# Loading wq with one transfer of 32 KB rows in place of two of 16 KB rows, and issuing the output store from ScalarE

## The chip, the cores and the metric

The kernel runs on one core of a Trainium2 chip. The metric is device time in microseconds (us), the median of several executions; lower is better. "Span" is the profiled part of one execution, about 1.9 us shorter than the device time.

In the profiles PE is the matmul unit of TensorE, DVE is VectorE, ACT ScalarE and SP SyncE; q1, q8 and q10 are the DMA queues of SyncE, of the instructions and of ScalarE. A wait marked "issue" is one for nothing that the profile shows. A stretch is called warm where TensorE's granted clock is full, and cold where it is half.

## The reference, cut to what matters

One decode step of a conditioned transformer block for 4 sequences: six modulation vectors from `c` and `w_mod`, layer norm, a q projection, attention of 32 query heads over the last 1024 positions of 8 key/value heads, an output projection, then a feed-forward block.

```python
mod = (silu(c) @ w_mod).reshape(4, 6, 1, 512)         # w_mod 512 x 3072, 3 MB
h = layernorm(x) * (1 + ca) + sa
q = h @ wq                                            # wq 512 x 4096, 4 MB
p = softmax(q @ k.T * 128 ** -0.5)                    # k, v: 8 MB each
x = x + ga * ((p @ v) @ wo)                           # wo 4096 x 512, 4 MB
h = layernorm(x) * (1 + cb) + sb
x = x + gb * (relu(h @ w1) @ w2)                      # w1, w2: 1.8 MB each
```

Nearly all of it is 32 MB of bfloat16 that is read once.

## The kernel before

All large loads go out from SP (SyncE) in the order in which they are needed. The parts that matter here, with cuts:

```python
for gi in range(KAHEAD):                  # KAHEAD = 2: k0, k1
    load_k(gi)
wmod_sb = wts.tile([P, DT, 6 * D], bf16, tag="med", name="wmod_sb")
nc.sync.dma_start(out=wmod_sb[:], in_=w_mod.rearrange("(p t) n -> p t n", t=DT))
wq_sb = wts.tile([P, DT, Hq * Dh], bf16, tag="big", name="wq_sb")
wq_src = A_wq.rearrange("(p t) n -> p t n", t=DT)
for t in range(0, DT, 2):
    nc.sync.dma_start(out=wq_sb[:, t:t + 2, :], in_=wq_src[:, t:t + 2, :])
for gi in range(KAHEAD, NG):              # k2 .. k7
    load_k(gi)
# ... v0 .. v7, wo in four, w1, w2 in five transfers

for t in range(DT):                       # q projection, 128 matmuls; t = 0, 1 read the first half
    for hq in range(Hq):
        nc.tensor.matmul(out=qT_v[:, hq, :], lhsT=wq_sb[:, t, hq * Dh:(hq + 1) * Dh], rhs=hT[:, t, :],
                         start=(t == 0 and hq == 0), stop=(t == DT - 1 and hq == Hq - 1))
# ... scores of k0, k1; transposes and scores of k2 .. k7; softmax; p @ v; wo; feed-forward
nc.vector.tensor_tensor(out=res[:], in0=zg[:], in1=x12_ps[:], op=ALU.add)
nc.sync.dma_start(out=out.rearrange("b o (g n) -> (o g) b n", g=NH), in_=res[::BS, :])
```

The transfers take their completion semaphores from a ring of eight. So each transfer from the ninth on waits until the one eight places before it has landed, and the issue times on SP show landings.

## Time and profile before

| | before |
|---|---|
| device time, median (lowest to highest) | 85.89 us (85.84 to 86.03, 3 runs) |
| span | 84.0 us |
| DMA queue of SP: bytes, share of 16 engines | 31.99 MB, 91.9% |
| PE, VectorE, ScalarE busy | 68%, 31%, 28% |
| last landing, as the start of the last matmuls of z | 80.16 us |
| res ready to the end of the span | 2.60 us |

The lines for the load stream, the chain and q are in the prediction below. The first is the page's row of TensorE's granted clock (one digit for each of 40 slices of 2.1 us, in tenths of full speed):

```profile
PEclk9999999858955555999999995795555555555555
```

The clock falls to half (5) near 18 us. The store in the timeline of SP (start, duration):

```profile
81.47 0.69 SPq L483 DMA_DIRECT2D out_dram<-res  x1
```

### The profile page before, as it was taken

Reading aid. Unit: us, or ns where it says so; the run is one execution under the profiler, and the core shown is the slowest. Engines: PE = TensorE matmul, PEld = TensorE weight load, DVE = VectorE, ACT = ScalarE, POOL = GpSimd, SP = SyncE. Lnnn points to the kernel's source line nnn. Section 1 sums busy time; section 2 is a strip of 40 time slices with the busy share of each in tenths; the row PEclk is TensorE's granted clock in tenths of the full one; section 3 lists DMA queues with packets and bytes.
Section 4 is the critical chain, followed back from the end, with each engine's and each line's share of the span. In section 5 each row is a group of like instructions: output and inputs, shape, how many; then the busy total and the mean of one; then the engine's idle time right before and its main releaser. Section 6 shows DMA issues by size and latency. Waiting matters only on the chain.

```text
span 84.0 us, 2368 instructions
## 1 busy us (share of the span) xinstructions
PE 57.2 (68%) x1064; PEld 46.8 (56%) x1064; DVE 26.3 (31%) x73; ACT 23.5 (28%) x37; POOL 5.2 (6%) x20
## 2 busy tenths in 40 slices
PE   0039930599629899999999239996455478598730
PEld 0039920238529749977777039996452058588510
DVE  0145470030430103654666677500003020241320
ACT  2314760003020004977789096300000010011000
POOL 6980000000000000000000000000000000000000
PEclk9999999858955555999999995795555555555555
DMA  0999998999989999999999999999999999999600
GB/s 2 329 406 452 456 480 374 429 444 429 437 374 417 417 441 409 409 413 433 425 406 413 425 429 417 409 425 429 413 409 413 429 419 443 417 376 401 236 4 2
DMA packets 4221, 32.14 MB, mean 382 GB/s; under 512 B 492, under 2 KB 628, under 8 KB 1140
## 3 DMA queue, kind: packets, MB, share of 16 engines
q1 hardware_dynamic: 4196, 31.99, 91.9%
q8 instruction: 8, 0.13, 0.6%
q10 hardware_dynamic: 16, 0.01, 0.0%
q14 instruction: 1, 0.01, 0.0%
HBM read 31.99 MB, written 0.00 MB: 381 GB/s over the span
## 4 chain that ended last, share of the span: by engine, by line
DMA 92%; SPq 2%; PE 1%; DVE 1%; issue 0%
DMA v<-in_A_v_cache_dram 28%; DMA wo_sb<-in_A_wo_dram 24%; DMA wq_sb<-in_A_wq_dram 21%; DMA w<-in_B_w_dram 19%; SPq L81 1%; PE z_ps L470 1%; SPq L90 1%; DVE zg L480 0%; DVE res L482 0%
## 5 line engine op out<-in xcount | busy, mean ns | idle before, releaser
L207 ACT COPY kT<-ktp 128x1024 bf16<-128x1024 bf16 x16 | 15.5, 1016 | 12.7 <-PE ktp L202 11.7
L202 PEld LDWEIGHTS <-k 128*128 128x128 bf16 x256 | 17.0, 108 | 3.7 <-issue 2.5
L202 PE MATMUL ktp<-ident_k,k 128*128 128x128 bf16 x256 | 18.0, 238 | 1.1 <-DMA k<-in_A_k_cache_dram 1.1
L205 DVE COPY kT<-ktp 128x1024 bf16<-128x1024 bf16 x16 | 11.1, 691 | 11.1 <-PE ktp L202 10.8
L340 PE MATMUL oT_ps<-pT,v 128*128 128x16 bf16 x256 | 7.3, 172 | 2.5 <-issue 1.9
L340 PEld LDWEIGHTS <-v 128*128 128x128 bf16 x256 | 7.1, 100 | 2.7 <-issue 2.0
L214 PE MATMUL sc_ps<-kT,qpad 128*32 128x512 bf16 x64 | 5.6, 445 | 0.4 <-DVE qpad L306 0.4
L357 PE MATMUL pT_ps<-ident_bf,p_rep 128*128 128x128 bf16 x32 | 3.3, 289 | 2.9 <-DVE p_rep L351 2.9
L357 PEld LDWEIGHTS <-p_rep 128*128 128x128 bf16 x32 | 2.9, 135 | 3.4 <-DVE p_rep L351 3.2
L236 PE MATMUL m_ps<-wmod_sb,siluT 128*32 128x512 bf16 x16 | 1.5, 516 | 4.5 <-DMA wmod_sb<-in_w_mod_dram 4.5
L302 PE MATMUL qT_ps<-hT,wq_sb 128*128 128x4 bf16 x128 | 3.6, 166 | 1.4 <-DVE ab L295 1.4
L302 PEld LDWEIGHTS <-wq_sb 128*128 128x128 bf16 x128 | 3.5, 104 | 1.5 <-issue 1.5
L409 ACT COPY y<-y_ps 128x256 f32<-128x256 f32 x1 | 0.4, 372 | 11.4 <-DVE y L408 11.4
L404 PE MATMUL y_ps<-wo_sb,o 128*32 128x512 bf16 x16 | 2.1, 620 | 2.0 <-DMA wo_sb<-in_A_wo_dram 1.1
L177 PE MATMUL tp<-ident_bf,cx_sb 8*128 8x8 bf16 x4 | 0.3, 167 | 4.5 <-DMA cx_sb<-in_A_x_dram 4.5
L236 PEld LDWEIGHTS <-siluT 128*32 128x32 bf16 x16 | 0.4, 107 | 4.8 <-issue 4.6
L382 DVE TENSOR_TENSOR oT_sb<-oT_ps,rb 128x128 bf16<-128x128 f32 x1 | 0.3, 292 | 8.6 <-PE oT_ps L340 8.6
L416 PEld LDWEIGHTS <-wo_sb 128*128 128x128 bf16 x64 | 2.5, 120 | 0.6 <-DMA wo_sb<-in_A_wo_dram 0.6
L416 PE MATMUL y_ps<-o,wo_sb 128*128 128x4 bf16 x64 | 2.4, 173 | 0.5 <-DMA wo_sb<-in_A_wo_dram 0.5
L351 DVE TENSOR_TENSOR p_rep<-e_sb,mi 128x512 int32<-128x512 int32 x4 | 2.5, 686 | 0.7 <-ACT e_sb L346 0.7
L470 PE MATMUL z_ps<-w,uT 128*32 128x128 bf16 x56 | 2.2, 302 | 0.7 <-DMA w<-in_B_w_dram 0.5
L177 PEld LDWEIGHTS <-cx_sb 8*128 8x128 bf16 x4 | 0.2, 108 | 4.5 <-issue 4.5
(107 smaller groups left out, 56.1 us busy)
## 6 DMA issues: line engine op xcount, KB each, us to landing
k<-in_A_k_cache_dram SPq DMA_DIRECT2D x8, 1024.0 KB, 26.2
v<-in_A_v_cache_dram SPq DMA_DIRECT2D x8, 1024.0 KB, 19.9
wq_sb<-in_A_wq_dram SPq DMA_DIRECT2D x2, 2048.0 KB, 20.7
wo_sb<-in_A_wo_dram SPq DMA_DIRECT2D x4, 1024.0 KB, 19.9
wmod_sb<-in_w_mod_dram SPq DMA_DIRECT2D x1, 3072.0 KB, 13.5
w<-in_B_w_dram SPq DMA_DIRECT2D x1, 1792.0 KB, 21.7
w<-in_B_w_dram SPq DMA_DIRECT2D x2, 512.0 KB, 19.2
w<-in_B_w_dram SPq DMA_DIRECT2D x1, 384.0 KB, 17.8
```

The lines of the kernel that those rows point to most:

```text
L202: nc.tensor.transpose(out=tp[:, ii, :], in_=k_tiles[gi][:, iq * IQ + ii, :], identity=ident_k)
L205: nc.vector.tensor_copy(out=dst, in_=tp[:])
L207: nc.scalar.copy(out=dst, in_=tp[:])
L214: nc.tensor.matmul(out=sc_ps[hw * CG:(hw + 1) * CG, half * HALF:(half + 1) * HALF], lhsT=qpad[:, b, par, hw, :], rhs=kT[:, half * (NI // 2 ...
L236: nc.tensor.matmul(out=m4_ps[k * CG:(k + 1) * CG, :], lhsT=siluT32[:, t, :], rhs=wmod_sb[:, t, k * D:(k + 1) * D], start=(t == 0), stop=(t ...
L302: nc.tensor.matmul(out=qT_v[:, hq, :], lhsT=wq_sb[:, t, hq * Dh:(hq + 1) * Dh], rhs=hT[:, t, :], start=(t == 0 and hq == 0), stop=(t == DT ...
L340: nc.tensor.matmul(out=oT_ps[:, hw, par].rearrange("p b r -> p (b r)"), lhsT=v_tiles[h][:, i, :], rhs=pT[:, i, c0:c0 + B * rep], start=(fi ...
L351: nc.vector.tensor_tensor(out=p_w[:, ws, :], in0=e_w[:, ws].unsqueeze(2).to_broadcast([P, WQ // 2, B]), in1=mi4[:].unsqueeze(1).to_broadca ...
L357: nc.tensor.transpose(out=tp[:, ii, :], in_=p_rep[:, i // 2, :, i % 2], identity=ident_bf[:])
L404: nc.tensor.matmul(out=y4_ps[q0:q0 + CG, :], lhsT=o4[:, l, g % 2, g // 2, :], rhs=wo_sb[:, g, l, :], start=(g == 0 and l < 4), stop=(g == ...
L416: nc.tensor.matmul(out=y_ps[:, m, :], lhsT=wo_sb[:, g, l, m::DT], rhs=o4[:, l, g % 2, g // 2, 0:B], start=False, stop=(g == NP - 1 and l = ...
L470: nc.tensor.matmul(out=z_ps[nh * CG:(nh + 1) * CG, :], lhsT=uT32[:, m, :], rhs=w2_sb[:, m, nh * DH2:(nh + 1) * DH2], start=(m == 0), stop= ...
```

## The change

The intent: larger rows mean fewer pieces for the DMA engines and one issue less on SP; and ScalarE, idle at the end, issues the store.

```diff
-    for t in range(0, DT, 2):
-        nc.sync.dma_start(out=wq_sb[:, t:t + 2, :], in_=wq_src[:, t:t + 2, :])
+    nc.sync.dma_start(out=wq_sb[:], in_=wq_src)
...
-    nc.sync.dma_start(out=out.rearrange("b o (g n) -> (o g) b n", g=NH), in_=res[::BS, :])
+    nc.scalar.dma_start(out=out.rearrange("b o (g n) -> (o g) b n", g=NH), in_=res[::BS, :])
```

Lines after the edit move up by one: L302 of the kernel before is L301 of the changed one.

## The prediction

> **What bounds the kernel now.** I read the row of 40 slices and the queue totals first, then the chain of waits in order of time, then the waits of the DMA queue, then the timelines around wq and at the end.
>
> ```profile
> DMA  0999998999989999999999999999999999999600
> ...
> q1 hardware_dynamic: 4196, 31.99, 91.9%
> q8 instruction: 8, 0.13, 0.6%
> ```
>
> The 16 DMA engines are busy in every slice from the second to the 37th. 91.9% of 84.0 us is 77.2 us of packet time, and it lies between 2.0 us (first k tile) and 80.0 us (last piece of w2), so there is hardly any hole in the stream. PE, at 68%, is not the bound.
>
> ```profile
> 2.71 17.78 DMA wq_sb<-in_A_wq_dram
> ...
> 20.50 23.76 DMA v<-in_A_v_cache_dram
> ...
> 44.28 19.86 DMA wo_sb<-in_A_wo_dram
> ...
> 64.16 15.96 DMA w<-in_B_w_dram
> ...
> 80.16 0.64 PE z_ps L470 x10
> ...
> 80.83 0.30 DVE zg L480
> ...
> 81.15 0.29 DVE res L482
> ```
>
> This is the chain that ended last: four stretches of the load stream, 77.4 us, then the last ten matmuls, two VectorE operations and the store. So only two things can move the end: how long the load queue takes for its 32 MB, and what happens after the last load has landed (80.12 us) until 84.0 us. Both parts of the change touch one of these, each by little.
>
> The size of a row's own cost comes from the issue times on SP. A load waits for the one eight places before it in the order of issue, so a start shows a landing:
>
> ```profile
> 8.30 0.54 SPq L81 DMA_DIRECT2D k<-in_A_k_cache_dram  x1
> 15.60 0.54 SPq L81 DMA_DIRECT2D k<-in_A_k_cache_dram  x1
> 20.50 0.54 SPq L101 DMA_DIRECT2D v<-in_A_v_cache_dram  x1
> 26.89 0.54 SPq L101 DMA_DIRECT2D v<-in_A_v_cache_dram  x1
> 54.22 0.33 SPq L119 DMA_DIRECT2D w<-in_B_w_dram  x1
> 56.70 0.33 SPq L125 DMA_DIRECT2D w<-in_B_w_dram  x1
> ```
>
> These are six answers of the timeline of SP (start, duration). The first four are released by k1, wmod, the first wq half and the second wq half; the last two by v4 and v5.
>
> **What the Trainium skill says.** (1) "DMA: Bandwidth & Descriptors", section "Issuing engines are not separate DMA queues": transfers from ScalarE and SyncE run on the same 16 engines, and another issuer only saves the sequencer's issue time. The trace agrees as far as it goes: the two small loads of ScalarE are its own queue (q10, 16 packets), and the engines are one pool. At the end SP's sequencer is idle, waiting 12.3 us for res, so there is no issue time to save. (2) The same page, "Latency and other measured facts", gives about 600 ns for the first byte of such a transfer. In the trace the store's issue ends at 82.16 us and its first packets begin in 82.70 to 82.80 us: about 0.6 us, agreed. (3) "Perfetto Trace Analysis", "DMA Instruction — HWDGE (DVE, Sync)": the profiled span of an issue is the wait for the descriptor generator's lock, its use, and the push of semaphores, and data movement is not in it. The store's 0.69 us is such a span. (4) "TensorE: Matmul & The Clock Gate", Part 1: the clock is at half until about 3.4 us of steady work. The trace shows a clock of 0.50 from 23 to 33.8 us and 1.00 after. This bears on a delay of PE below.
>
> **Part 1, wq in one transfer.** Removed: one issue on SP (two issues took 1.07 us together, one should take about 0.55), 128 of 256 row packets, one semaphore write per engine. The bytes stay.
>
> An engine carries 128/16 = 8 rows of each transfer. From the starts: v4 to v5 is 56.70 - 54.22 = 2.48 us for 8 rows of 8 KB, 310 ns a row. The first wq half is 20.50 - 15.60 = 4.90 us for 8 rows of 16 KB, 612 ns a row. wmod is 15.60 - 8.30 = 7.30 us for 8 rows of 24 KB, 912 ns. So 8 KB more costs some 301 ns, and about 10 ns is the row's own. One row of 32 KB is then 310 + 3 x 301 = 1213 ns against 2 x 612 = 1224 ns. Saved per engine: 8 x 11 = 0.09 us, and with one semaphore write less some 0.1 us. As the stream has no holes this comes off every later landing, down to the last of w2: -0.1 us on the path.
>
> The 0.5 us of SP issue is not on the path: the third, fourth and later loads are issued while k0 is still moving (k0 and k1 land at about 5.5 and 8 us; wq is issued at 2.7 us and starts to move only when wmod is through, after 15 us).
>
> The order of issue is otherwise the same. v0 now waits for wmod and not for the first wq half, so it goes out some 5 us earlier, and everything from v1 on waits for the same load as before. The queue holds seven or eight loads, some 18 us of work, so neither matters.
>
> **What part 1 costs PE.** Before, the 64 q matmuls of t=0,1 read the first half and run while the second half arrives:
>
> ```profile
> 25.20:26.90 1.70, 1.70 (x64) 1.70 (x64) 0.50 0.99 414
> 26.90:28.80 1.90, 1.88 (x70) 1.80 (x67) 0.50 0.99 414
> ```
>
> These two stretches are of line 302 only. The second half is seen landed at 26.89 us, exactly when the 65th matmul begins. With one semaphore for 4 MB none may start before about 26.8 us. So the q projection runs 26.8 to 30.4 us in place of 25.2 to 28.8: PE's whole chain is 1.6 us later. If the warm clock comes a window later too, up to 3.4 us more run at half clock, 1.7 us lost, 3.3 us in all. I looked for where this is given back:
>
> ```profile
> PE oT_ps L340 <- issue: 1.9, 1, 1.9
> PE y_ps L404 <- DMA wo_sb<-in_A_wo_dram: 1.1, 1, 1.1
> ...
> PE oT_ps L340 <- DMA v<-in_A_v_cache_dram: 0.6, 1, 0.6
> ```
>
> Between 58 and 67 us PE is idle 1.9 us before v6's work, 0.6 us for v7 and 1.1 us for the second piece of wo, 3.6 us together. After it wo, w1 and w2 pace PE anew (0.5, 0.4 and 0.3 us of waits), so the end does not see the delay. The k tiles' buffers come free later too, but v5 (issued at about 36.9 us) needs k2's transposes, done by about 33.5 us; and a late issue would eat from a queue of 18 us.
>
> **Part 2, the store from ScalarE.** Before: res is done at 81.44 us, the issue begins at 81.47 and takes 0.69 us, packets begin 0.6 us later, and the program ends at 84.0. The issue, the flight and the closing barrier (2.5 us) are all on the path. ScalarE's last operation starts at 75.73 us, so it is idle and waits there. Its own issues in this trace are these:
>
> ```profile
> 0.73 0.55 ACTq L71 DMA_DIRECT2D cx_sb<-in_c_dram  x1
> 1.31 0.26 ACTq L72 DMA_DIRECT2D cx_sb<-in_A_x_dram  x1
> ```
>
> They are of a simpler pattern (4 rows against the store's 16 pieces in three dimensions), so they do not prove a cheaper issue. SP takes 0.54 us for loads with three dimensions and 0.33 us for the late ones with two, so the duration follows the pattern more than the issuer. My estimate for ScalarE is 0.4 to 0.8 us, middle 0.6: -0.1 us, with 0.3 us of doubt either way. SP still waits for the store's semaphore at the end, so the barrier is as before.
>
> **Sum.** -0.1 (rows and semaphore) - 0.1 (issue) + 0 (PE's delay absorbed) = -0.2 us: 85.89 becomes 85.7 us, 0.2% faster.
>
> **Rivals.** *PE's delay reaches the end.* For it: the slack at the end is small, 0.3 + 0.2 us before the last matmuls of z. Against it: 3.6 us of idle PE lies between. If half were passed on, +0.8 us: 86.6 us. I give it 5%. *Larger packets slow the stream or meet an instruction fetch badly.* Eight fetches share the engines (q8), and one comes at 21 to 23 us, in wq. A 32 KB row holds an engine 1.2 us in place of 0.6, so a fetch or PE's next instructions could come 0.6 us later. Against: 24 KB rows of wmod ran at the best rate of all. It would make +0.1 to +0.6 us on wq's landing, which PE hides: 85.8 to 86.1 us. *Larger rows are much faster.* It would have to be seen in wmod: 24 KB rows are 2% better per byte than 8 KB rows, so 4 MB that gain 0.9% are 0.09 us. Against it is the whole trend. *ScalarE's path is slower* (semaphore wait, first use of its queue since 1.3 us): +0.3 us, 86.1 us, 15%.
>
> **Range and chances.** The three runs before lie within 0.2 us. Adding 0.3 us of doubt for the store, 0.1 for the stream and some for a delay passed on, 8 in 10 lie in 85.3 to 86.2 us. A gain of 2% would be 1.7 us, more than issue and flight of the store together with all that the rows save: 0.02. A loss of 2% needs the whole delay of PE at the end: 0.02. Within 2%: 0.96.
>
> **What would show each step.** Right: SP's timeline shows one wq issue of about 0.55 us; what waited for the second wq half starts at about 26.8 us; L302 starts then and not at 25.2, waiting for wq; the idle stretches of PE at 58 to 67 us shrink by 1.6 to 3.3 us; the last landing is 80.0 us against 80.12; q1 has some 144 packets fewer; the store is an ACTq row of 0.4 to 0.8 us. Wrong: the wait before the last matmuls of z is gone and PE is late there; the last landing moves by more than 0.3 us; or the store's issue to end differs from 2.5 us by more than 0.4 us.

## More of the kernel before

At the end SP waits for the eight semaphores in a fixed order before it closes the program.

## The result, and the profile after

| | runs | median | ratio to before, 95% interval |
|---|---|---|---|
| before, same rounds | 6 | 85.84 us (85.76 to 86.03) | |
| changed | 6 | 85.88 us (85.76 to 86.0) | 1.0003 [0.9988, 1.0018] |

A ratio is the mean time of one kernel's fast runs over that of the other's of the same rounds, so not quite the ratio of the medians.

The chain of waits of the changed kernel, in order of time (start, duration, what):

```profile
2.04 13.62 DMA wmod_sb<-in_w_mod_dram
...
15.68 28.53 DMA v<-in_A_v_cache_dram
...
44.23 19.87 DMA wo_sb<-in_A_wo_dram
...
64.11 15.93 DMA w<-in_B_w_dram
...
80.08 0.66 PE z_ps L469 x12
...
80.76 0.30 DVE zg L479
...
81.09 0.29 DVE res L481
```

wq is no longer named, since v0 is now released by wmod. The form is the same: four stretches of loads to 80.04 us, then the tail. The last landing is seen 0.08 us earlier than before (80.04 against 80.12 us).

The issue of wq, and the issue that its landing releases (timeline of SP, changed kernel):

```profile
2.67 0.44 SPq L93 DMA_DIRECT2D wq_sb<-in_A_wq_dram  x1
...
26.83 0.54 SPq L100 DMA_DIRECT2D v<-in_A_v_cache_dram  x1
```

One issue, and wq seen landed at 26.83 us, where the second half was seen landed at 26.89 us. The packets in the trace give the rows' cost: the median is 312 ns for 8 KB, 611 ns for 16 KB, 912 ns for 24 KB, and 1213 ns for the 32 KB rows of the changed kernel. A 32 KB row is one packet, and costs 9 ns less than two of 16 KB.

The store, from ScalarE (timeline of ACT, changed kernel), and the clock and queue rows of its page:

```profile
81.41 0.60 ACTq L482 DMA_DIRECT2D out_dram<-res  x1
```

```profile
PEclk9999997555555555899999997598555555555555
...
q1 hardware_dynamic: 4032, 31.98, 91.7%
```

The issue is 0.60 us in place of 0.69. q1 has 164 packets fewer than before: 128 rows, 16 semaphore writes, and the store's 20 packets, which are in q10 now. The clock is at half for the whole time from 14 to 34 us in this execution. Whether the change did that is asked below. It made PE late for a reason of its own:

```profile
27.31 3.56 PE L301 MATMUL qT_ps<-hT,wq_sb 128*128 128x4 bf16 x128 [1.41 <-DVE ab L294]
```

The q projection starts 2.1 us later than before (25.20 us), and what it waited for last was VectorE's inputs, not wq. Yet the last matmuls of z still wait for loads, and the end did not move.

### The profile page after: what moved, and what is told of

Read it like the earlier page. It is cut to its first block, busy times and chain, and to the rows that moved or that the text cites. A ratio compares the mean times of both kernels' runs of the same rounds, so it can differ in the third digit from the quotient of the medians.

```text
span 84.0 us, 2367 instructions
## 1 busy us (share of the span) xinstructions
PE 59.3 (71%) x1064; PEld 48.8 (58%) x1064; DVE 26.5 (31%) x73; ACT 23.6 (28%) x37; POOL 5.2 (6%) x20
## 4 chain that ended last, share of the span: by engine, by line
DMA 93%; SPq 1%; PE 1%; DVE 1%; issue 0%
DMA v<-in_A_v_cache_dram 34%; DMA wo_sb<-in_A_wo_dram 24%; DMA w<-in_B_w_dram 19%; DMA wmod_sb<-in_w_mod_dram 16%; SPq L81 1%; PE z_ps L469 1%; DVE zg L479 0%; DVE res L481 0%
## 5 line engine op out<-in xcount | busy, mean ns | idle before, releaser
L206 ACT COPY kT<-ktp 128x1024 bf16<-128x1024 bf16 x16 | 15.5, 1015 | 12.7 <-PE ktp L201 11.6
L301 PE MATMUL qT_ps<-hT,wq_sb 128*128 128x4 bf16 x128 | 3.6, 166 | 1.4 <-DVE ab L294 1.4
L301 PEld LDWEIGHTS <-wq_sb 128*128 128x128 bf16 x128 | 3.5, 104 | 1.5 <-DMA wq_sb<-in_A_wq_dram 1.5
```

The lines of the kernel that those rows point to most:

```text
L206: nc.scalar.copy(out=dst, in_=tp[:])
```

## The experiments

Twelve runs were made. The first four went together on one chip, and so did the next four and the last four; each group has its own runs of the kernel before.

### wq in one transfer, the store left on SP

```diff
-    nc.scalar.dma_start(out=out.rearrange(...), in_=res[::BS, :])
+    nc.sync.dma_start(out=out.rearrange(...), in_=res[::BS, :])
```

(against the changed kernel)

> wq in one transfer, the store left on SP. Theory A (each part is worth a tenth of a microsecond or less): the last load lands about 0.08 us earlier, SP's issue of the store is again about 0.69 us, and because the store now counts on the semaphore that is second to last in SP's list of closing waits, one wait of 0.06 us follows its landing; so 0.0 to 0.1 us faster, span 83.95 to 84.05 us. Rival B (the two parts are each large and cancel): 0.3 us or more faster, or slower, here and the opposite in the run with the store alone.

Measured: 85.80 us median of 6, against 85.93 us of 11 runs of the kernel before; ratio 0.999 [0.9977, 1.0004]. Span 84.00 us. Theory A holds; a large effect that the store's part cancels is excluded.

### The store from ScalarE, wq left in two transfers

```diff
-    nc.sync.dma_start(out=wq_sb[:], in_=wq_src)
+    for t in range(0, DT, 2):
+        nc.sync.dma_start(out=wq_sb[:, t:t + 2, :], in_=wq_src[:, t:t + 2, :])
```

(against the changed kernel)

> wq left in two transfers, the store from ScalarE. Theory A: last landing as before (80.1 us), issue about 0.60 us in place of 0.69, the store's semaphore is the last of the closing waits as before, so no 0.06 us behind it: 0.05 to 0.1 us faster, span 83.95 to 84.0 us. Rival B: 0.3 us or more slower or faster. A second rival (the issuer makes no difference and 0.60 against 0.69 is chance): issue 0.65 to 0.72 us, time as before.

Measured: 85.86 us median of 6; ratio 0.9992 [0.9978, 1.0005]. Span 84.08 us, slightly over what was expected, because the loads landed later in this execution (last matmuls of z at 80.24 us). The store in the timelines of the two halves, wq alone first:

```profile
81.36 0.69 SPq L482 DMA_DIRECT2D out_dram<-res  x1
```

```profile
81.55 0.60 ACTq L483 DMA_DIRECT2D out_dram<-res  x1
```

The issue follows the issuer: 0.69 us in all four profiles with SP, 0.60 to 0.61 us in all nine with ScalarE. What of it reaches the end is in the table after the looks.

### The changed kernel again

> The changed kernel once more, beside its two halves. Theory A: ratio 0.998 to 1.001, span 83.9 to 84.05, wq seen landed at about 26.8 us, and the start of the q projection set by the TensorE clock of that run: 26.8 us where the stretch from 17 to 23 us ran mostly warm, 27.3 us where it ran at half clock. Rival: the q projection is late because of the change itself, and starts at 27.3 us or later whatever the clock.

Measured: 85.89 us median of 6; ratio 0.9998 [0.9984, 1.0011]; span 84.08 us. q projection at 27.35 us, clock again at half from 14 to 34 us. The execution that was profiled was cold, so the two theories on q's start were not told apart here.

### wq in pieces of 2 KB

```diff
-    wq_sb = wts.tile([P, DT, Hq * Dh], bf16, tag="big", name="wq_sb")
+    wq_sb = wts.tile([P, DT * Hq * Dh // 1024, 1024 + 32], bf16, tag="big", name="wq_sb")
-    nc.sync.dma_start(out=wq_sb[:], in_=wq_src)
+    nc.sync.dma_start(out=wq_sb[:, :, 0:1024], in_=A_wq.rearrange("(p t) (u n) -> p (t u) n", t=DT, n=1024))
-            nc.tensor.matmul(out=qT_v[:, hq, :], lhsT=wq_sb[:, t, hq * Dh:(hq + 1) * Dh], rhs=hT[:, t, :],
+            nc.tensor.matmul(out=qT_v[:, hq, :], lhsT=wq_sb[:, (t * Hq + hq) // 8, hq % 8 * Dh:(hq % 8 + 1) * Dh], rhs=hT[:, t, :],
```

> The changed kernel with wq still in one transfer, but written into a tile with a gap after every 2 KB, so that it moves in 16 pieces of 2 KB per partition in place of one of 32 KB. Result correct. Theory A (a piece costs some 10 ns of its engine of its own and the stream has no holes, so it comes off or onto the end one to one): a 2 KB packet took 84 ns before, so 16 take 1.35 us against 1.21 us, times 8 rows per engine: 1.1 us more, time 86.7 to 87.2 us. Rival (the row length of wq is hidden by something else): within 0.2 us of the kernel before. PE idles longer before the q projection, which must not show beyond the 1.1 us.

Measured: correct, 86.76 us median of 4 (86.73 to 86.78); ratio 1.0101 [1.0085, 1.0117]. Against the changed kernel of the same chip (85.89 us) that is +0.87 us. The chain of this run has the last matmuls of z here:

```profile
81.02 0.67 PE z_ps L469 x12
```

The landing is 0.85 us later than the 80.17 us of the changed kernel's run on the same chip, and the time 0.87 us longer: what the row count costs the stream comes out at the end one to one. Of the 1.05 us that the packet times give (16 x 84 - 1213 = 131 ns, times 8 rows per engine) four fifths arrive; neighbouring small packets overlap somewhat in the trace (from 17 to 21 us the packet times add up to 1.05 of the 16 engines' time, in the changed kernel to 1.00). So the mechanism of part 1 is real, and in the change itself it is small because 9 ns times 8 is small.

A side effect in the timeline of SP:

```profile
3.29 14.74 SPq L81 DMA_DIRECT2D k<-in_A_k_cache_dram  x1
```

The issue after wq (k2) held SP's sequencer for 14.74 us, where it takes 0.54 us otherwise. The stream had enough queued not to suffer.

### Half of wq's bytes

```diff
-    nc.sync.dma_start(out=wq_sb[:], in_=wq_src)
+    nc.sync.dma_start(out=wq_sb[:, 0:2, :], in_=wq_src[:, 0:2, :])
-            nc.tensor.matmul(out=qT_v[:, hq, :], lhsT=wq_sb[:, t, hq * Dh:(hq + 1) * Dh], rhs=hT[:, t, :],
+            nc.tensor.matmul(out=qT_v[:, hq, :], lhsT=wq_sb[:, t % 2, hq * Dh:(hq + 1) * Dh], rhs=hT[:, t, :],
```

> The changed kernel with only the first half of wq loaded, in one transfer, and used twice; the result is wrong on purpose. 2 MB less move, 4.9 us of stream. Theory A (the stream sets the end, and PE follows some 3 us behind it): after 58 us PE waits for loads, in the profile of the changed kernel, 0.45 + 0.49 + 0.40 + 0.35 + 0.15 us, in that of the kernel before 0.6 + 1.1 + 0.5 + 0.4 + 0.5 us, so PE becomes the bound after 2 to 3 us are taken off: 2 to 3.5 us faster. But wq would land some 5 us earlier too, and PE then starts the q projection when hT is ready, at 25 to 27 us as now. Rival (only the load queue counts): 4.9 us faster, about 81 us.

Measured: four runs of 81.1, 81.3, 82.33 and 83.67 us, with mean granted clocks of 0.745, 0.755, 0.732 and 0.716; before 85.98 us. The two fastest count as fast (ratio 0.9446 [0.9422, 0.947], 4.8 us less), the other two, with the lower clocks, as slow. By the fast runs my number for theory A (2 to 3.5 us) missed, and the pure load queue (4.9 us) was met within 0.2 us; of the slow runs one lies in theory A's range (2.3 us less) and one just outside it (3.65 us). The profile is of the 82.33 us run, a slow one. In it PE's waits from 50 us on name no load; these are the two longest:

```profile
PE pT_ps L356 <- DVE p_rep L350: 2.9, 1, 2.9
PE oT_ps L339 <- issue: 1.7, 1, 1.7
```

In this run the last load landed at 75.18 us (80.04 in the changed kernel) and PE ended its last matmuls only at 77.27 us: PE and its clock set the end. The fast runs left no trace. An estimate for them: from the last landing to the end the changed kernel takes 3.97 us, so loads alone would end this kernel at 75.18 + 3.97 = 79.15 us of span, and the fast runs have spans of 79.2 and 79.4 us. So the load stream is the bound, with a margin over PE that depends on the clock. (The output still passed the comparison, though half of wq was not used: that check doesn't see this error.)

### k2, and k2 with k3, ahead of wq

```diff
+    for gi in range(KAHEAD, KAHEAD + 1):      # + 2 in the second kernel
+        load_k(gi)
     nc.sync.dma_start(out=wq_sb[:], in_=wq_src)
-    for gi in range(KAHEAD, NG):
+    for gi in range(KAHEAD + 1, NG):          # + 2 in the second kernel
```

> The changed kernel with k2 loaded ahead of wq: the same transfers, but wq lands 2.5 us later, at 29.3 us, and the q projection with it. It asks how much delay of PE the end can take. Theory A (the idle of 1.9 us at 58 us is a stall for instructions that moves along with PE, and only waits for loads give way): slack is 0.45 + 0.49 + 0.40 + 0.35 + 0.15 = 1.8 us beyond a start at 27.3 us, so a start at 29.3 us costs 0 to 0.7 us: 85.8 to 86.6 us. The prediction's own account (3.6 us of slack by 67 us beyond a start at 25.2 us, and more waits after it): no change, 85.8 to 86.0 us.

> The same with k2 and k3 ahead of wq: wq lands at 31.8 us, the q projection starts 4.5 us later than in the changed kernel. Theory A: 4.5 - 1.8 = 2.7 us on the end, less up to 1 us where the TensorE clock happens to be warm: 87.5 to 88.9 us. The prediction's own account (3.6 us and the 1.2 us of waits after it, from a start at 25.2 us): 6.6 - 4.8 = 1.8 us or less: up to 87.6 us. Rival (the end is the load queue alone): 85.9 us.

Measured: with k2 first 85.81 us median of 4, ratio 0.9988 [0.9969, 1.0006]; with k2 and k3 first 88.34 us, ratio 1.0271 [1.0245, 1.0296]. Every load is the same, only PE is delayed: the q projection starts at 29.19 and 31.82 us. The chain of waits of the first of them:

```profile
3.25 25.90 DMA wq_sb<-in_A_wq_dram
...
29.19 3.59 PE qT_ps L303 x128
```

From there to the end that chain is PE and what it feeds. PE's waits from 61 us on, in the same kernel:

```profile
PE oT_ps L341 <- issue: 1.2, 1, 1.2
PE y_ps L405 <- DVE o L396: 0.9, 1, 0.9
...
PE z_ps L471 <- DVE uT L466: 0.2, 1, 0.2
```

No wait for a load is left: this kernel ends as early as the changed one with all of its slack used up. Another 2.63 us of delay cost 2.53 us (88.34 against 85.81). From a start at 25.2 us the end can take about 4 us of delay: 31.82 - 25.20 = 6.62 us of delay cost 88.34 - 85.98 = 2.36 us, so 4.3 us were absorbed, somewhat more or less with the clock (of the four runs with k2 and k3 first, the one at a mean clock of 0.732 took 88.01 us, the three at 0.68 took 88.33 to 88.49). With k2 first, both accounts were right (theory A from 0 to 0.7 us). With k3 too, theory A's 87.5 to 88.9 us holds, and the prediction's account of the slack (87.6 us at most) falls: it counted 1.9 us of idle as slack, of which 1.2 and 1.4 us are still there in these two kernels, where PE waits for no load any more.

That idle is the one marked "issue" in the work on v. It ended at nearly the same distance from the start of a 16 KB packet of the instruction queue (q8), here in five profiles:

| kernel | packet starts | PE resumes | between | idle of PE |
|---|---|---|---|---|
| before | 57.48 | 60.04 | 2.56 | 1.92 |
| changed | 59.01 | 61.45 | 2.44 | 1.55 |
| changed again | 59.31 | 61.79 | 2.48 | 1.84 |
| k2 first | 61.70 | 64.10 | 2.40 | 1.18 |
| k2, k3 first | 64.33 | 66.93 | 2.60 | 1.39 |

It moves with PE by 6.9 us and shrinks by 0.5 to 0.7 us (without that delay the other profiles have 1.43 to 1.95 us). In all fourteen profiles it begins after 190 of the 256 matmuls on v, two before v6's first one, so it is no wait for v6, and it ends 2.35 to 2.63 us after such a packet begins. That is what waiting for instructions would look like. It wasn't isolated by an experiment, so the name of the wait stays an inference; that most of it isn't slack is shown.

### The store from GpSimd

```diff
-    nc.scalar.dma_start(out=out.rearrange(...), in_=res[::BS, :])
+    nc.gpsimd.dma_start(out=out.rearrange(...), in_=res[::BS, :])
```

> The changed kernel with the store issued by GpSimd[...]. Theory A (the time from res to the end of the program is issue plus flight, and follows the issuer): the page on DMA gives about 1 us to the first byte on this path in place of 0.6, so some 0.3 to 1.2 us slower, 86.1 to 87.1 us. Rival (the store's path is covered by something else at the end): within 0.15 us.

Measured: 86.30 us median of 4; ratio 1.0037 [1.0017, 1.0057], 0.3 us slower, within theory A's range. The store in its timeline:

```profile
81.53 0.70 POOL L482 DMA_DIRECT2D out_dram<-res  x1 [75.49 <-DVE res L481]
```

It begins 0.30 us after res (81.23 us), not 0.03, and res to the end takes 3.11 us in place of 2.63. Of this 0.48 us, 0.33 lie before the landing: the issue begins 0.27 us later and takes 0.09 us longer. The other 0.15 us lie after it: here three of SP's closing waits follow the landing (83.29 us), in the changed kernel one (these waits are explained after the looks). The page that the expectation means is "DMA: Bandwidth & Descriptors" of the Trainium skill, "Latency and other measured facts"; its later first byte is not what this trace shows: the first packets begin 1.27 us after the start of the issue, with ScalarE 1.25 and with SP 1.29. So the store's path is on the end and does follow the issuer, though not for the reason that was expected; SP and ScalarE are merely close to each other.

### Four more looks

The changed kernel and the kernel before, twice each, one run and one profile.

> A further profile of the changed kernel, for two things that one profile leaves open. Clock phase: the time at which TensorE's clock changes differs from run to run, and every profile of a kernel with one wq transfer so far had half clock from 14 to 34 us. If the phase is chance, some look will show a warm stretch near 20 us, and then the q projection starts at about 26.8 us, waiting for wq (the prediction's claim); otherwise at 27.2 to 27.4 us, waiting for hT. Accounts: last landing 80.0 to 80.15 us, res to the end of the program 2.62 to 2.64 us.

> As the look before it: q projection at 26.8 us in a warm phase or at 27.3 us in a cold one; last landing 80.0 to 80.15 us; res to the end 2.62 to 2.64 us.

> A further profile of the kernel before. If the clock phase is chance and not the change's doing, one of these looks may show half clock from 14 to 34 us here too, and then the q projection starts at about 27.3 us with both halves of wq landed. Accounts: last landing 80.1 to 80.2 us, res to the end 2.59 to 2.61 us, SP's issue of the store 0.68 to 0.69 us.

> As the look before it: the q projection at 25 to 25.6 us in a warm phase, 27.3 us in a cold one; last landing 80.1 to 80.2 us; res to the end 2.59 to 2.61 us.

Measured: 86.02 and 85.84 us changed, 86.17 and 86.11 us before, 85.90 us for the shared run of before; single runs. The expected landings were missed in three of the four looks (80.27 us changed; 80.47 and 80.41 before), so landings scatter more than I had thought; res to the end was met in all four. The second look at the changed kernel fell in a warm phase (half clock from 15.5 to 18.9 us only, then warm to 22.3 us). Its timeline from 24.9 us on:

```profile
25.01 0.18 DVE L291 TENSOR_TENSOR hT<-hx,modT 128x16 bf16<-128x16 f32 x1
...
26.89 0.54 SPq L100 DMA_DIRECT2D v<-in_A_v_cache_dram  x1
...
26.92 0.72 PE L301 MATMUL qT_ps<-hT,wq_sb 128*128 128x4 bf16 x21 [3.00 <-DMA wq_sb<-in_A_wq_dram]
```

hT was ready at 25.19 us, wq landed at 26.89, and the first q matmul began at 26.92 us. The first look at the kernel before fell in a cold phase (half clock from 14.4 to 34.9 us), and its q projection looks like this:

```profile
27.51 0.65 PE L302 MATMUL qT_ps<-hT,wq_sb 128*128 128x4 bf16 x19 [1.41 <-DVE ab L295]
```

So both phases occur with either form of the load, and the change is not needed for a late start of q; what PE does before q reads nothing of wq. That the change leaves the odds of the phases alone is not shown: 3 of the 4 profiles with two transfers have a warm stretch from 20 to 21.8 us, and 2 of the 10 with one. The phase alone moves q's start from 25.2-25.6 to 27.5 us in kernels with two transfers. With one transfer the start is 26.9 us in a warm phase and 27.1 to 27.35 us in the others (in the first look at the changed kernel, too, q waited for wq: hT ready at 26.43 us, wq landed at 27.08, q at 27.11).

The two terms of the tail, over all profiles of these four variants. Packet time is that of SP's queue over 16 engines, from the trace:

| variant (profiles) | packet time, us | last matmuls of z start, us | res to end, us |
|---|---|---|---|
| before (3) | 77.18 to 77.24 | 80.16, 80.45, 80.51 | 2.60, 2.60, 2.61 |
| store from ScalarE (1) | 77.22 | 80.24 | 2.56 |
| one wq transfer (1) | 76.94 | 80.04 | 2.67 |
| changed (4) | 76.98 to 77.07 | 80.08, 80.14, 80.17, 80.31 | 2.62 to 2.63 |

The store from ScalarE makes the tail 0.04 us shorter, half of what its issue saves: its packets begin 0.65 us after the end of the issue (0.60 with SP). One wq transfer makes it 0.06 us longer. The cause is in the records of SP's closing waits, here of the kernel before and of the changed one (start in us, semaphores waited for; number 110 is the store's before, 109 after):

```
          kernel before             changed kernel
82.460    109, 105                  83.129    109, 105  <- the store has landed
83.226    110, 106  <- landed       83.189    110, 106
83.294    next step                 83.256    next step
```

With one transfer less, the store takes the seventh semaphore of the ring and not the eighth, and SP has one more wait of 0.06 us to run after the landing. Both terms together: -0.04 + 0.06 = +0.02 us, and the four profiles of the changed kernel show +0.02 to +0.03.

## Why the prediction was right

The outcome was forecast right: within 2%, 85.88 us in the range of 85.3 to 86.2 us. That range holds the time of the kernel before as well, so the outcome alone tests little; the steps do:

**What bounds the kernel.** Right. Pieces of 2 KB lengthened the stream by 0.85 us and the time by 0.87 us. Half of wq's bytes took off 4.8 of 4.9 us in the fast runs, and less where the clock was lower.

**Rows and semaphore, -0.1 us.** Right in mechanism and about right in size. The row cost that was extrapolated, 1213 ns, is what the trace shows. Packet time fell by about 0.19 us (means of the four profiles with two transfers and the five with one: 77.2 and 77.0 us) and the last landing by about 0.2 us on average, more than the 8 x 9 ns that the rows explain. But the landings of one kernel scatter by 0.35 us, so I do not claim the rest. (q1 has 164 packets fewer and not 144, since the store's 20 went to q10; the prediction left them out.)

**The issue from ScalarE, -0.1 us.** The step that was mis-sized, though it was given 0.3 us of doubt. "My estimate for ScalarE is 0.4 to 0.8 us, middle 0.6" was exact (0.60 us), but only 0.04 of the 0.09 us arrived, as the flight became longer. And "SP still waits for the store's semaphore at the end, so the barrier is as before" was wrong by 0.06 us: removing a transfer from the queue moved the store within SP's list of waits. I had seen that order of issue shifts, and not asked what it does to the last transfer.

**The sum, -0.2 us.** Not confirmed: both intervals of the changed kernel (down to 0.9988 and to 0.9984) leave out 0.9977. The 14 runs of the changed kernel since the prediction have a mean of 85.89 us and a standard deviation of 0.09; the 27 of the kernel before, 85.93 and 0.12, over several chips and with the single runs. The profiles' account is -0.2 + 0.02 us with a scatter about as large. A gain of 0.2 us is excluded; between 0 and -0.1 us nothing here decides, and nothing depends on it.

**PE's delay.** "L302 starts then and not at 25.2, waiting for wq" is right for a warm phase (26.92 us, waiting 3.0 us for wq) and moot where hT comes later than wq, as it did in two of the four profiles of the changed kernel. The prediction treated the clock of one profile as the kernel's. It also read that clock slightly wrong: the half clock ended at 33.2 us, not 33.8. And PE was at work from q's start on, yet the clock stayed at half for another 8.0 us (6.8 to 9.7 us over the fourteen profiles), so the 3.4 us of its point (4) do not describe this stretch. That PE's delay is given back by 67 us is right: in the changed kernel the wait for the second piece of wo fell from 1.1 to 0.4 us, and the second half of its p @ v ran without a wait for v7. Work on that piece of wo begins at 66.61 us, where it began at 66.66 before. But the reckoning of 3.6 us was wrong in one term: of the 1.9 us before v6's work at least 1.2 are no slack. What holds is about 4 us in all, including the later waits for wo, w1 and w2.

**The rivals.** PE's delay did not reach the end in this change, and does when it is 2.6 us longer than all of the slack. The larger packets met the instruction fetch no worse than the smaller ones: in wq one engine of 16 finished some 1.4 us after the other 15 in the kernel before (26.39 against 24.9 us) and in the changed one (26.34 against 24.97 us). This lag is what q waits for in a warm phase: in the second look at the changed kernel 15 engines had reported wq by 25.28 us, about when hT was ready (25.19 us), and the last one at 26.87 us. So nearly all of the 1.6 us that the single transfer cost PE there came from one engine. With two transfers the same lag falls on the second half, while q works on the first. An instruction packet of 0.98 us and a row of 1.72 us in place of 1.21 add up to the lag; that they sat on this engine is inferred, as the trace does not name the engine of a packet.

## What to carry to other kernels

When the DMA engines are busy without holes, a change of row length is worth its packets times their own cost, here 8 to 13 ns, divided over 16 engines: reckon it before trying it, and look for bytes and not for rows where rows are as long as here (a 24 KB row took 912 ns, three of 8 KB 936). Merging two loads into one takes away the early start on the first, and makes the first work wait for the slowest of the 16 engines; whether that is free is a question of slack, and slack is idle that waits for a load, not every idle stretch. One profile shows one phase of TensorE's clock; before a difference of 2 us in PE's schedule is put down to a change, look at a second one.

## What the Trainium skill lacked or had wrong

- "DMA: Bandwidth & Descriptors": it gives no time of a row against its length for loads from SyncE (its measured table goes by the size of a transfer from GpSimd). Here, medians of one packet: 2 KB 84 ns, 8 KB 312, 16 KB 611, 24 KB 912, 32 KB 1213. A row of 32 KB goes as one packet.
- The same page, "Issuing engines are not separate DMA queues", says that issuing from several engines at once only saves the sequencer's time, and does not speak of a lone store at the end. There the issuer is on the path: res to the end took 2.60 us from SP and 2.56 from ScalarE; with one closing wait behind the landing 2.67 and 2.63; from GpSimd, with three such waits, 3.11.
- No page that I read tells how long an issue can hold its sequencer when the transfer ahead has many pieces: 14.74 us in place of 0.54, behind a transfer of 16 pieces per partition.
- "Runtime: NRT & Kernel Launch", "Instruction fetch mechanics", calls the crossing of a 16 KiB block of instructions mostly hidden. Here PE stood idle for 1.2 to 1.95 us in each of fourteen profiles, ending 2.35 to 2.63 us after such a packet began; that it waited for instructions is an inference. The packets took 0.96 to 1.25 us each (611 ns for data of that size).
